# Weights in runs of four and a half rows: a decode kernel with attention and a small MLP, w3 loaded ahead of wq

## The chip, the core and the metric

The kernel runs on one core of a Trainium2 chip. Its engines are PE (TensorE: matrix products; PEld is its weight load), DVE (VectorE), ACT (ScalarE), POOL (GpSimd) and SP (SyncE, which here only issues DMA transfers); 16 DMA engines move the data. The metric is the device time of one execution in microseconds (us). It was measured three times for the kernel before, and one execution was profiled.

## The reference

Four sequences decode one token each. With D = 576, 32 query heads, 16 key/value heads of 128, F = 4608:

```python
x = A_x                                   # (4, 1, 576)
xn = _layernorm(x)
q = xn @ wq                               # (4, 4096): 32 heads of 128
k, v = last 2048 rows of the caches       # each (4, 16, 2048, 128), two query heads share one
A = softmax(q k^T * 128**-0.5) v @ wo     # (4, 576)
h = gelu(_layernorm(xn) @ w1)             # shifted by one or two tokens; with S = 1 that leaves zeros
x1 = xn + shifted(h) @ w2
B = x1 + gelu(_layernorm(x1) @ w3) @ w4   # w3: 576 x 4608, w4: 4608 x 576
out = x + A + B
```

All tensors are bfloat16. K and V are 33.6 MB each, the weights together 21.4 MB.

## The kernel before, in words

Each engine has its own program. The function add puts an operation into an engine's list with a key; each list is sorted by key, and semaphores carry the waits. So the order on an engine is set by the keys, and one late operation holds up all that are behind it. SP's list holds all transfers but x and the output, and a transfer that waits holds up those behind it too. Once issued, transfers run in the order of the queue, each split over the 16 DMA engines.

**SP's order.** wq in two transfers (keys -50, -49), w1, w2 and w3 in two each (-48 to -46), the first 24 of 36 rows of w4 (-45), then 16 K chunks of 2 MB (0 to 15), 8 V chunks of 4 MB, the rest of w4, and wo in five parts. K chunks go through a ring of four slots: chunk c waits until chunk c - 4 has been transposed (L296). Chunks 2 and 3 wait for q instead, since wq lies in their slots. V chunks 0 and 1 overwrite w3 and w4 and wait for MO0, the first part of the last MLP product. Later V chunks and wo wait for the products of V chunks that lay in their place.

**The weights before the change.** 576 rows don't divide by 128 partitions. The first 512 rows of wq, w1, w2 and w3 come as four rows in one run per partition (a run of 32 KB for wq, 36 KB for w3). The last 64 rows (rag_src, L209) come as 128 half rows in a transfer of their own (4 KB, 576 B, 576 B and 4.6 KB a run). x is transposed to match: four transposes of every fourth element (L334), and two more from ragsrc (L337), which holds the last 64 elements with zeros between them, once for the even partitions (first half of the columns) and once for the odd (second half).

**PE's order** (keys): q_zero; the transposes of xn and of its second layer norm; q (L370, 40 matmuls of four stationary columns, four side by side in column groups of the array, over two banks); the transposes of q (L383); the hidden layer (L404, two column groups); the product with w2 (L412, L413, two halves, the second waiting for DVE's sum of the first); the transposes of the third layer norm (L334); t1 (L431); a zero fill of banks (L358); h2 = x1n @ w3 (L444 and L450, three groups of 24 matmuls, waiting for w3); its transposes (L459); MO0 (L397, waiting for w4's first part); a zero fill of the score banks (L344). Then the loop over K: 64 transposes (L506) a chunk and 16 score matmuls (L513), with DVE (L490) and ACT (L489) copying the transposed blocks out. After it come the softmax, the loop over V (L574), and the products with w4's rest and wo (L397).

**DVE and ACT** in the prologue: the layer norms (ln_ops, L313; statistics, ACT's square root at L319, the scaling at L323, the two copies into ragsrc at L325 and L327), the copies of transposed x (L351, L426), of q (L376 on DVE, L377 on ACT) and into Qpad (L391), the sums x1 (L418), the gelus (L422, L423, L465), the copies of the transposed h2 (L468, L469) and of MO0 (L482, L483).

Of the kernel before, what the change touches and what calls it, by code (L numbers as in the profile page):

```python
# [37 lines left out]
def bass_parallel_sum__sliding_block_cached__mixer_s_mlp__decode_kernel(  # L38
# [32 lines left out]
    with ExitStack() as ctx:  # L71
# [6 lines left out]
        kring = sb("kring", [128, 4 * UE], BF16)  # L78
        vring = sb("vring", [128, 5 * UE], BF16)
        ktb = sb("ktb", [128, NKT * 1024], BF16)  # L80
        PT_t = sb("PT", [128, NT * 32], BF16)
# [6 lines left out]
        wqmain = kring[:, 2 * UE:4 * UE].rearrange("p (r n) -> p r n", r=4)  # L88
        wqrag = PT_t[:, 0:Hq * Dh // 2]
        w3main = vring[:, 0:4 * F].rearrange("p (r n) -> p r n", r=4)  # L90
        w4t = [vring[:, a:a + n * D].rearrange("p (r n) -> p r n", r=n) for a, n in ((4 * F, W4P[1]), (4 * UE, W4R - W4P[1]))]
        assert 4 * F + W4P[1] * D <= 4 * UE and (W4R - W4P[1]) * D + 1024 <= UE
# [9 lines left out]
        w1main = cut(4 * D).rearrange("p (r n) -> p r n", r=4)  # L102
        w1rag = cut(HALF)
        w2main = cut(4 * D).rearrange("p (r n) -> p r n", r=4)
        w2rag = cut(HALF)
        w3rag = cut(FH)
# [5 lines left out]
        PTv = PT_t[:].rearrange("p (q t b e) -> p q t b e", q=NVS, t=NTV, b=NPAIR)  # L112
# [9 lines left out]
        xn2_bf = sb("xn2_bf", [B, D], BF16)  # L122
        x1_bf = sb("x1_bf", [B, D], BF16)
        x1n_bf = sb("x1n_bf", [B, D], BF16)
        ragsrc = sb("ragsrc", [B, 3, 2, 128], BF16)
        xnT = sb("xnT", [128, 6, B], BF16)
        xn2T = sb("xn2T", [128, 6, B], BF16)
        x1nT = sb("x1nT", [128, 6, B], BF16)
        hs_inT = sb("hs_inT", [128, 6, B], BF16)
        hh_sb = sb("hh_sb", [32 + B, HALF], BF16)  # L130
        h2_sb = sb("h2_sb", [128, 3, 384], BF16)
        q_sb = vring[:, 5 * UE - 1024:5 * UE].rearrange("p (k x) -> p k x", k=2)
# [36 lines left out]
        Qps = [ps[:, 4, :], ps[:, 6, :]]  # L169
        QTps = ps[:, 0, :].bitcast(BF16).rearrange("p (k n j x) -> p k n j x", k=2, n=4, j=4)  # L170
        HSps = ps[0:B, 5, 0:HALF]
        HHps = [ps[32 * k:32 * k + B, 3, 0:HALF] for k in range(2)]
        H2ps = [ps[:, 4 + k, 0:384] for k in range(3)]
        H2Tps = [ps[:, k, :].bitcast(BF16).rearrange("p (n j x) -> p n j x", n=8, j=4) for k in range(2)]
        XTps = [ps[:, k, 0:12].bitcast(BF16).rearrange("p (c b) -> p c b", b=B) for k in range(3)]
# [33 lines left out]
        def rag_src(w_ap):  # L209
            return w_ap[512:576, :].rearrange("r (h n) -> (r h) n", h=2)  # L210
# [29 lines left out]
        P(lambda e: e.memset(ragsrc[:], 0.0), sig="rag_zero", key=-97)  # L240
# [24 lines left out]
        def mask_of(t, tag, view):  # L265
            add("dve", lambda e: e.tensor_reduce(out=t[:], in_=view, axis=AX.X, op=ALU.add), waits=["ident_f"], sig=tag, key=-8)
        mask_of(maskd, "maskd", ident_f[:].rearrange("p (t y) -> p t y", t=2))
# [45 lines left out]
        def ln_ops(idx, src, dst, first_waits, tag, k0):  # L313
# [9 lines left out]
            add("dve", lambda e: e.tensor_scalar(out=dst[:], in0=src[:], scalar1=mv[:, idx, 0:1], scalar2=rstd[:, idx:idx + 1],  # L323
                                                 op0=ALU.subtract, op1=ALU.mult), waits=[f"{tag}_rstd"], sig=f"{tag}_n", key=k0 + 0.04)
            add("dve", lambda e: e.tensor_copy(out=ragsrc[:, idx, 0, 0:128:2], in_=dst[:, 512:D]),  # L325
                waits=[f"{tag}_n"] + (["rag_zero"] if idx == 0 else []), key=k0 + 0.05)
            add("dve", lambda e: e.tensor_copy(out=ragsrc[:, idx, 1, 1:128:2], in_=dst[:, 512:D]),  # L327
                waits=["qpad_zero"] if idx == 1 else [], sig=tag, key=k0 + 0.05)

        def pe_xT(src, idx):  # L330
            def f(e):
                v = src[:, 0:512].rearrange("b (p r) -> b r p", r=4)
                for r in range(4):
                    e.transpose(XTps[idx][:, r, :], v[:, r, :], ident_bf[0:B, 0:B])  # L334
                ins = None
                for h in range(2):
                    ins = e.transpose(XTps[idx][:, 4 + h, :], ragsrc[:, idx, h, :], ident_bf[0:B, 0:B])  # L337
                return ins
            return f

# [7 lines left out]
        ln_ops(1, xn_bf, xn2_bf, ["ln1"], "ln2", -30)  # L348
        for idx, (src, tag, dst) in enumerate(((xn_bf, "ln1", xnT), (xn2_bf, "ln2", xn2T))):
            add("pe", pe_xT(src, idx), waits=["ident_bf", tag], sig=f"xT{idx}", key=-50 + idx)  # L350
            add("dve", lambda e, dst=dst, idx=idx: e.tensor_copy(out=dst[:], in_=XTps[idx]), waits=[f"xT{idx}"], sig=f"xnT{idx}",  # L351
                key=-29 + idx * 0.1)
# [8 lines left out]
        add("pe", pe_bank0(Qps), waits=["zeros_bf"], sig="q_zero", key=-51)  # L361

        def pe_q(r):
            def f(e):
                ins = None
                for k in range(8):
                    w, x_ = (wqmain[:, r, 512 * k:512 * (k + 1)], xnT[:, r, :]) if r < 4 else \
                        (wqrag[:, 512 * (k % 4):512 * (k % 4 + 1)], xnT[:, 4 + k // 4, :])
                    j = k % 4
                    ins = e.matmul(Qps[k // 4][32 * j:32 * j + B], lhsT=x_, rhs=w, start=False, stop=(r == 4),  # L370
                                   tile_position=(0, 32 * j), skip_group_check=True)
                return ins
            return f
        for r in range(5):
            add("pe", pe_q(r), waits=[ev_wq[r // 4], "xnT0"], sig="q" if r == 4 else f"q_{r}", key=-30 + r)
        add("dve", lambda e: e.tensor_copy(out=q_sb[:, 0], in_=Qps[0]), waits=["q"], sig="q_sb0", key=-11)  # L376
        add("act", lambda e: e.activation(out=q_sb[:, 1], in_=Qps[1], func=ACTF.Copy), waits=["q"], sig="q_sb1", key=-20)  # L377

        def pe_qT(k):
            def f(e):  # L380
                ins = None
                for n in range(4):
                    ins = e.transpose(QTps[:, k, n].rearrange("p j x -> p (j x)"), q_sb[:, k, 128 * n:128 * (n + 1)], ident_bf[:])  # L383
# [358 lines left out]
```

## Time and profile before

| | us |
|---|---|
| median of 3 runs | 214.5 (214.28 to 214.53) |
| the profiled execution | 214.28 |
| its span | 213.0 |
| PE busy | 170.8 (80%) |
| DVE busy | 118.6 (56%) |
| ACT busy | 61.3 (29%) |
| SP queue's packets, share of 16 DMA engines | 97.7% |
| bytes read | 88.49 MB |

The span runs from the first instruction of the program to the last; the time is 1.3 us longer. All positions are us from the span's start. A row of the timeline has the start, the duration, the engine, the line, the operation with out<-in and its count, and in brackets the idle time before it and what ended that. The chain of waits has start, duration and what it was. In a windows row stand the stretch, its length, then the busy time of PE, PEld, DVE, ACT and POOL with instruction counts, the clock granted to PE, the DMA engines' share and GB/s. A queue row has packets, MB, and the share of 16 engines' time.

### The profile page before, as it was taken

The numbers are of one execution on the slowest core, as the hardware profiler recorded it, in microseconds if no ns is written. First come the engines' busy times: TensorE is split into PE (matmuls) and PEld (weight loads), VectorE is DVE, ScalarE is ACT, GpSimd is POOL, SyncE is SP. The second block draws the span as 40 slices with busy tenths as digits, with TensorE's granted clock in tenths as the row PEclk, the third lists the DMA queues.
The fourth block names the chain that finished last, engine by engine and source line by source line (L and its number), as shares of the span: only waits on it lengthen the run. The fifth ranks groups of instructions, "written<-read, shape, count | busy, mean of one in ns | idle before, by whom it ended". The sixth has DMA issues, their size and how long they took to land.

```text
span 213.0 us, 4861 instructions
## 1 busy us (share of the span) xinstructions
PE 170.8 (80%) x2207; PEld 131.5 (62%) x2211; DVE 118.6 (56%) x172; ACT 61.3 (29%) x72; POOL 16.6 (8%) x39
## 2 busy tenths in 40 slices
PE   2037438679999999999999923899999869899965
PEld 0013106458877887778788802598888656788732
DVE  4964500047777776766676756999674570610110
ACT  2001402026666666655566645100000000000000
POOL 8993000000000000000000000000000000000000
PEclk9999757999999999999999985999999996999999
DMA  7999999999999999999999999999999999999993
GB/s 278 412 379 511 422 379 425 430 428 420 418 440 421 428 431 428 421 431 434 426 428 468 418 425 455 397 455 421 412 455 415 437 443 406 418 431 420 431 416 134
DMA packets 5786, 88.65 MB, mean 416 GB/s; under 512 B 648, under 2 KB 1040, under 8 KB 1808
## 3 DMA queue, kind: packets, MB, share of 16 engines
q1 hardware_dynamic: 5760, 88.49, 97.7%
q8 instruction: 8, 0.13, 0.3%
q14 instruction: 2, 0.02, 0.0%
q10 hardware_dynamic: 16, 0.01, 0.0%
HBM read 88.49 MB, written 0.00 MB: 415 GB/s over the span
## 4 chain that ended last, share of the span: by engine, by line
DMA 64%; PE 24%; DVE 9%; ACT 1%; issue 1%; SPq 0%
DMA kring<-in_A_k_cache_dram 40%; DMA vring<-in_A_wo_dram 12%; DMA vring<-in_A_v_cache_dram 12%; PE ps L574 11%; PE ps L506 7%; DVE xn_bf L323 4%; PE ps L513 2%; PE ps L370 2%; DVE vring L541 1%; DVE rmax L519 1%; DVE ktb L566 1%; PE ps L535 1%; DMA x_sb<-in_A_x_dram 1%; ACT ktb L489 0%; DVE stats L314 0%
## 5 line engine op out<-in xcount | busy, mean ns | idle before, releaser
L490 DVE COPY ktb<-ps 128x1024 bf16<-128x1024 bf16 x80 | 53.8, 690 | 24.5 <-PE ps L506 24.1
L506 PEld LDWEIGHTS ps<-perm_bf,kring 128*128 128x128 bf16 x1024 | 57.2, 98 | 11.6 <-issue 9.1
L506 PE MATMUL ps<-perm_bf,kring 128*128 128x128 bf16 x1024 | 62.6, 219 | 1.8 <-DMA kring<-in_A_k_cache_dram 1.1
L489 ACT ACTIVATE ktb<-ps 128x1024 bf16<-128x1024 bf16 x48 | 49.2, 1024 | 31.5 <-PE ps L506 30.5
L566 DVE TENSOR_TENSOR ktb<-PT,mH_bf 128x4096 bf16<-128x4096 bf16 x16 | 36.2, 2288 | 14.5 <-PE ps L574 14.5
L574 PE MATMUL ps<-vring,ktb 128*128 128x256 bf16 x256 | 30.3, 282 | 4.2 <-DMA vring<-in_A_v_cache_dram 3.3
L574 PEld LDWEIGHTS ps<-vring,ktb 128*128 128x128 bf16 x256 | 25.7, 101 | 8.3 <-issue 3.4
L574 PE MATMUL ps<-kring,ktb 128*128 128x256 bf16 x256 | 28.6, 273 | 0.9 <-DMA kring<-in_A_v_cache_dram 0.9
L574 PEld LDWEIGHTS ps<-kring,ktb 128*128 128x128 bf16 x256 | 25.0, 98 | 4.5 <-issue 1.2
L632 ACT ACTIVATE out_sb<-ps 4x288 bf16<-4x288 f32 x1 | 0.4, 400 | 76.3 <-PE ps L397 76.3
L513 PE MATMUL ps<-ktb,Qs 128*32 128x512 bf16 x272 | 17.8, 382 | 1.2 <-ACT ktb L489 1.2
L513 PEld LDWEIGHTS ps<-ktb,Qs 128*32 128x32 bf16 x272 | 5.8, 95 | 6.7 <-DVE ktb L490 1.3
L334 PE MATMUL ps<-ident_bf,xn_bf 4*128 4x4 bf16 x8 | 0.5, 169 | 11.2 <-DVE ragsrc L327 11.2
L535 PE MATMUL ps<-vring,pick_bf 128*32 128x256 bf16 x64 | 3.9, 411 | 6.4 <-DVE rinv L553 6.4
L592 DVE TENSOR_SCALAR tmp<-ps,maskd 128x128 f32<-128x128 f32 x2 | 0.7, 350 | 14.8 <-PE ps L574 14.8
L334 PEld LDWEIGHTS ps<-ident_bf,xn_bf 4*128 4x128 bf16 x8 | 0.4, 111 | 12.1 <-DVE ragsrc L327 8.7
L444 PE MATMUL ps<-vring,x1nT 128*4 128x384 bf16 x48 | 4.8, 486 | 3.7 <-DMA ktb<-in_B_w_dram 3.7
L323 DVE TENSOR_SCALAR xn_bf<-xn_bf,mv,rstd 4x576 bf16<-4x576 bf16 x1 | 7.1, 7102 | 0.0
L535 PEld LDWEIGHTS ps<-vring,pick_bf 128*32 128x32 bf16 x64 | 2.1, 118 | 8.2 <-DVE rinv L553 6.9
L468 DVE COPY h2T_sb<-ps 128x128 bf16<-128x128 bf16 x1 | 0.2, 226 | 12.4 <-PE ps L459 12.4
L246 POOL MEMSET ktb<- 128x8192 bf16 x1 | 6.9, 6925 | 0.0
L397 PE MATMUL ps<-vring,ORT 128*4 128x288 bf16 x64 | 4.6, 286 | 2.4 <-DMA vring<-in_A_wo_dram 2.2
(115 smaller groups left out, 87.1 us busy)
## 6 DMA issues: line engine op xcount, KB each, us to landing
kring<-in_A_k_cache_dram SPq DMA_DIRECT2D x16, 2048.0 KB, 14.7
vring<-in_A_v_cache_dram SPq DMA_DIRECT2D x4, 4096.0 KB, 24.6
kring<-in_A_v_cache_dram SPq DMA_DIRECT2D x3, 4096.0 KB, 34.0
vring<-in_B_w_dram SPq DMA_DIRECT2D x1, 4608.0 KB, 24.7
kring<-in_A_wq_dram SPq DMA_DIRECT2D x1, 4096.0 KB, 12.2
kring<-in_A_v_cache_dram SPq DMA_DIRECT2D x2, 2048.0 KB, 27.3
vring<-in_B_w_dram SPq DMA_DIRECT2D x1, 3456.0 KB, 34.7
vring<-in_A_wo_dram SPq DMA_DIRECT2D x1, 1872.0 KB, 30.4
```

What stands on the lines that cost most here:

```text
L246: P(lambda e: e.memset(ktb[:, NKT // 2 * 1024:NKT * 1024], 0.0), key=-92, inc=(("E", LB - 2), 1))
L323: add("dve", lambda e: e.tensor_scalar(out=dst[:], in0=src[:], scalar1=mv[:, idx, 0:1], scalar2=rstd[:, idx:idx + 1], op0=ALU.subtract, op ...
L370: ins = e.matmul(Qps[k // 4][32 * j:32 * j + B], lhsT=x_, rhs=w, start=False, stop=(r == 4), tile_position=(0, 32 * j), skip_group_check=True)
L397: return e.matmul(ACC[h], lhsT=lhsT, rhs=rhs, start=start, stop=stop, tile_position=(0, 32 * h), skip_group_check=True)
L444: ins = e.matmul(H2ps[k][32 * j:32 * j + B].rearrange("b (p t) -> b p t", t=3), lhsT=x1nT[:, r, :], rhs=w3main[:, r, :].rearrange("x (p t) ...
L489: return "act", lambda e: e.activation(out=ktbuf[:, n % NKT], in_=tb[n % 4], func=ACTF.Copy)
L490: return "dve", lambda e: e.tensor_copy(out=ktbuf[:, n % NKT], in_=tb[n % 4])
L506: ins = e.transpose(tb[j % 4][:, t, :], kslot_t(k)[:, 8 * kb + t, :], perm_bf[:])
L513: ins = e.matmul(Sps[32 * u:32 * u + 32, q, :].rearrange("p (t i) -> p t i", t=16), lhsT=Qs[:, k, 32 * u:32 * u + 32], rhs=ktgrp[:, (4 * k ...
L535: ins = e.matmul(ps[32 * j:32 * j + 32, 4 + qt, 256 * ih:256 * (ih + 1)].rearrange("p (t a e) -> p t a e", a=NPAIR, e=2), lhsT=pick_bf[:, ...
L566: return lambda e: e.tensor_tensor(out=PTpad[:, n % 4], in0=PTv[:, qt, NH * h:NH * (h + 1), bp, :].unsqueeze(2).to_broadcast([128, NH, NX, ...
L574: ins = e.matmul(ps[:, 0, 0:256], lhsT=PTpad[:, 2 * (k % 2) + h, 2 * g:2 * g + 2].rearrange("p t h e -> p (t h e)"), rhs=vslot(k)[:, Dh * ...
```

## The change

wq, w1, w2 and w3 come in one transfer each. 576 rows are 64 groups of nine, so a partition takes half a group: four and a half rows in one run (36 KB of wq, 5.2 KB of w1 and of w2, 41.5 KB of w3). In such a run the halves of a row lie in turn on even and odd places, the other way round on even and odd partitions. So each matmul runs over a half row (nine of them), with eight stationary columns of x: four with x on the even partitions and zeros on the odd, four the other way. The one set of four outputs is the first half of the columns, the other the second. xs holds these columns; two DVE operations write them from the transposed x with the mask par. x is first laid out in pairs (xp).

With that, q has 36 matmuls of eight columns into one bank instead of 40 of four into two, one copy (on ACT) and four transposes; the hidden layer 9 in one column group instead of 10 in two; the product with w2 9 + 9 instead of 5 + 5; h2 two groups of 36 (320 and 256 columns) instead of three of 24; and the transposition of h2 is 18 products with a slice of the identity instead of 9 transposes. ragsrc, its copies and its memset on POOL are gone.

On SP w3 goes first (key -50), then wq (-49), w1, w2 and w4. q's last part no longer has a transfer of its own to wait for. w4's first part starts a little later in its buffer, since w3 takes more of it. The buffer PT moves to the end of kring, and wq's runs reach into it.

```diff
-        def rag_src(w_ap):
-            return w_ap[512:576, :].rearrange("r (h n) -> (r h) n", h=2)
+        def runs(w_ap):
+            return w_ap.rearrange("(m e) n -> m (e n)", e=9).rearrange("m (a x) -> (m a) x", a=2)
...
-        ev_wq = [add_dma([(kring[:, 2 * UE:4 * UE], A_wq[0:512, :].rearrange("(p r) n -> p (r n)", r=4))], "wq", (), -50),
-                 add_dma([(wqrag, rag_src(A_wq))], "wqr", (), -49)]
-        ev_w1 = add_dma([(w1main, B_w1[0:512, :].rearrange("(p r) n -> p r n", r=4)), (w1rag, rag_src(B_w1))], "w1", (), -48)
-        ev_w2 = add_dma([(w2main, B_w2[0:512, :].rearrange("(p r) n -> p r n", r=4)), (w2rag, rag_src(B_w2))], "w2", (), -47)
-        ev_w3 = add_dma([(vring[:, 0:4 * F], B_w3[0:512, :].rearrange("(p r) n -> p (r n)", r=4)), (w3rag, rag_src(B_w3))],
-                        "w3", (), -46)
+        ev_wq = add_dma([(wq_t, runs(A_wq))], "wq", (), -49)
+        ev_w1 = add_dma([(w1_t, runs(B_w1))], "w1", (), -48)
+        ev_w2 = add_dma([(w2_t, runs(B_w2))], "w2", (), -47)
+        ev_w3 = add_dma([(w3_t, runs(B_w3))], "w3", (), -50)
...
+        def xs_ops(idx, k0):
+            for a in range(2):
+                add("dve", lambda e, a=a: e.tensor_scalar(
+                        out=xs_t[:, idx, 2 * B * (1 - a):2 * B * (11 - a)].rearrange("p (r v b) -> p r v b", v=4, b=B)[:, :, 0:4:3, :],
+                        in0=XTps[idx].unsqueeze(2).to_broadcast([128, 5, 2, B]), scalar1=par[:, a:a + 1], scalar2=None, op0=ALU.mult),
+                    waits=([f"xT{idx}"] + ([] if idx else ["par"])) if a == 0 else [], sig=f"xs{idx}{a}", key=k0 + 0.01 * a)
...
+        def pe_q(s_):
             def f(e):
                 ins = None
+                for j in range(4):
+                    ins = e.matmul(Qps[32 * j:32 * j + 2 * B], lhsT=x_at(0, s_), rhs=wq_t[:, NQ // 2 * s_ + 512 * j:NQ // 2 * s_ + 512 * (j + 1)],
+                                   start=False, stop=(s_ == 8), tile_position=(0, 32 * j), skip_group_check=True)
                 return ins
...
         def pe_hh(e):
             ins = None
+            for s_ in range(9):
+                ins = e.matmul(HHps, lhsT=x_at(1, s_), rhs=w1_t[:, HALF * s_:HALF * (s_ + 1)], start=(s_ == 0), stop=(s_ == 8))
             return ins
...
+                for s_ in range(9):
+                    w = w3_t[:, FH * s_:FH * (s_ + 1)].rearrange("x (p t) -> x p t", t=W4R)
+                    for j in range(4):
+                        ins = e.matmul(H2ps[k][32 * j:32 * j + 2 * B].rearrange("b (p t) -> b p t", t=n), lhsT=x_at(2, s_),
+                                       rhs=w[:, :, 9 * j + t0:9 * j + t0 + n], start=False, stop=(s_ == 8),
+                                       tile_position=(0, 32 * j), skip_group_check=True)
...
+            for k, (t0, n) in enumerate(TS):
+                for t in range(n):
+                    for g in range(2):
+                        ins = e.matmul(H2Tps[64 * g:64 * (g + 1), t0 + t], lhsT=h2_v[k].rearrange("q (p t) -> q p t", t=n)[:, :, t],
+                                       rhs=sel[:, :, B * g:B * (g + 1)], start=True, stop=True, tile_position=(0, 64 * g),
+                                       skip_group_check=True)
```

More of the change, by code (lines that the diff above doesn't have):

```diff
@@ L121, in bass_parallel_sum__sliding_block_cached__mixer_s_mlp__decode_kernel @@
         xn_bf = sb("xn_bf", [B, D], BF16)
-        xn2_bf = sb("xn2_bf", [B, D], BF16)
+        xp_bf = sb("xp_bf", [B, 3, 5 * 128], BF16)
         x1_bf = sb("x1_bf", [B, D], BF16)
[L124 to L132, printed above, removed]
+        xs_t = sb("xs", [128, 3, 22 * B], BF16)
+        par = sb("par", [128, 2], FP32)
+        hs_inT = sb("hs_inT", [128, 9, 2, B], BF16)
+        hh_sb = sb("hh_sb", [2 * B, HALF], BF16)
+        h2_sb = sb("h2_sb", [128, 64 * 9], BF16)
+        q_sb = vring[:, 5 * UE - 512:5 * UE]
         h2T_sb = sb("h2T_sb", [128, W4R, B], BF16)
@@ L347, in bass_parallel_sum__sliding_block_cached__mixer_s_mlp__decode_kernel @@
         ln_ops(0, x_sb, xn_bf, [ev_x], "ln1", -40)
[L348 to L352, printed above, removed]
+        ln_ops(1, xn_bf, None, ["ln1_n"], "ln2", -30)
+        for idx, tag in enumerate(("ln1", "ln2")):
+            add("pe", pe_xT(idx), waits=["ident_bf", tag], sig=f"xT{idx}", key=-50 + idx)
+            xs_ops(idx, -29 + idx * 0.1)
         def pe_bank0(banks):
@@ L360, in pe_bank0 @@
             return f
-        add("pe", pe_bank0(Qps), waits=["zeros_bf"], sig="q_zero", key=-51)
-        def pe_q(r):
+        add("pe", pe_bank0([Qps]), waits=["zeros_bf"], sig="q_zero", key=-51)
+        def pe_q(s_):
             def f(e):
                 ins = None
[L366 to L371, printed above, removed]
-                return ins
-            return f
@@ L374, in bass_parallel_sum__sliding_block_cached__mixer_s_mlp__decode_kernel @@
[L374 to L383, printed above, removed]
-                return ins
-            return f
```

138 lines of the change are left out of this document (64 added, 74 removed).

## Prediction

> **What bounds the kernel now.** I read the page first: the busy share of the DMA engines in 40 slices, then the queues.
>
> ```profile
> span 213.0 us, 4861 instructions
> ...
> DMA  7999999999999999999999999999999999999993
> ...
> q1 hardware_dynamic: 5760, 88.49, 97.7%
> q8 instruction: 8, 0.13, 0.3%
> ```
>
> From the second slice to the one before last the DMA engines are full. SyncE's queue (q1) moves 88.49 MB in 5760 packets, and their time is 97.7% of all that 16 engines have. PE comes second with 80%, so I ask next which of the two is waited for, in the chain of waits:
>
> ```profile
> 18.53 40.55 DMA kring<-in_A_k_cache_dram
> ...
> 59.12 1.51 PE ps L506 x24
> 60.63 0.98 PE ps L513 x16
> 61.61 2.35 PE ps L506 x40
> 63.96 0.02 issue
> 63.98 14.67 DMA kring<-in_A_k_cache_dram
> ...
> 185.11 25.35 DMA vring<-in_A_wo_dram
> ```
>
> The chain names long transfers, but in each of them the transfer spends most of its time queued behind others. A K chunk is issued at 63.98 and lands 14.67 us later, which is three chunks of 4.89 us: it stood behind two. PE needs 63.96 - 59.12 = 4.84 us for one. DMA is the bound, PE is 0.05 us a chunk faster, and no queue runs empty. The last piece of wo lands at 185.11 + 25.35 = 210.46, and the rest of the 213.0 is the end of the output.
>
> So two things can move the end: the time that the DMA engines need for their bytes and packets, and a hole in their work. One more view, the windows at the end, shows that the engines don't finish together:
>
> ```profile
> 209.00:210.00 1.00, 0.65 (x12) 0.35 (x10) 0.00 (x0) 0.00 (x0) 0.00 (x0) 1.00 0.51 203
> 210.00:211.00 1.00, 0.71 (x12) 0.26 (x8) 0.00 (x0) 0.00 (x0) 0.00 (x0) 1.00 0.12 40
> ```
>
> The last two columns are the DMA share and the GB/s: with shares of 0.51 and 0.12, half of the engines' work is over by about 209.5, the last of it at 210.5. The slowest engine sets the time, and the fastest are up to some 2 us ahead of it.
>
> **Part 1, the transfers.** The bytes stay. Four small transfers go (the last 64 rows of wq, w1, w2 and w3), each of 128 runs and 16 closing packets: 576 packets, 36 on each engine. What a packet costs beside its bytes I take from the queue rows of two stretches, 12 to 17.5 us (weights, small runs among them) and 60 to 80 us (K, 16 KB runs), and the rate from a window with 32 KB runs:
>
> ```profile
> q1 hardware_dynamic: 752, 2.44, 109.2%
> ```
> ```profile
> q1 hardware_dynamic: 583, 8.50, 100.0%
> ```
> ```profile
> 140.00:160.00 20.00, 19.95 (x181) 17.58 (x181) 17.11 (x8) 0.00 (x0) 0.00 (x0) 1.00 1.01 435
> ```
>
> At 435 / 16 = 27.2 bytes per ns, the first stretch has 1.092 x 16 x 5.5 = 96.1 us of engine time, of which the bytes need 89.7: 6.4 us over 752 packets, 8.5 ns each. The second has 320 us, the bytes 312.5: 13 ns each. 36 packets are then 0.31 to 0.46 us per engine. From below it may be nothing, since packets overlap (a share of 109.2%). From above: wq's large part lands at 13.0 (rows below) and w3's small one at 31.3 (L444 waits for it until 31.34). The 7.16 MB between take 16.5 us at 435 GB/s, so 1.85 us are lost there to everything: packets, seams, and an instruction fetch of 16 KB that falls into them. I take **0.35 us**, near the lower packet price, because the stretch with small runs is the nearest row.
>
> The Trainium skill (DMA: Bandwidth & Descriptors, Anatomy of one DMA) gives a fixed cost of about 2 us per DMA beside the bytes, and says that most of it is waiting for the completion. If it added up in a full queue, four fewer would be worth 8 us; the first row above speaks against that (2.44 MB in 5.5 us is 444 GB/s, though several transfers end there).
>
> **Part 2, w3 ahead of wq: when PE can start.** Everything that PE does before the K chunks now waits for wq behind w3. How late is that?
>
> ```profile
> 0.80 0.37 SPq L205 DMA_DIRECT2D kring<-in_A_wq_dram  x1
> ```
> ```profile
> kring<-in_A_wq_dram SPq DMA_DIRECT2D x1, 4096.0 KB, 12.2
> ```
>
> 4.19 MB landed at 0.80 + 12.2 = 13.0, as if full rate began at 3.4. w3 and wq are 10.03 MB: 23.0 us, so wq lands at about **26.4**. w1 and w2 follow by 29.5, w4's first part by 37.7, K chunk 0 before 44.5. The work of PE until the first K transposition, which was spread over two waits for DMA, now runs in one piece after 26.4. Its steps, from PE's timeline:
>
> ```profile
> 14.20 3.27 PE L370 MATMUL ps<-kring,xnT 128*4 128x512 bf16 x32
> 17.30 0.60 PE L370 MATMUL ps<-PT,xnT 128*4 128x512 bf16 x8
> 18.70 0.62 PE L383 MATMUL ps<-ident_bf,vring 128*128 128x128 bf16 x8 [0.81 <-DVE vring L376]
> 19.26 0.78 PE L404 MATMUL ps<-ktb,xn2T 128*4 128x288 bf16 x10
> 19.87 0.65 PE L412 MATMUL ps<-ktb,hs_inT 128*4 128x288 bf16 x4
> ...
> 26.48 1.14 PE L358 MATMUL ps<-zeros_bf 128*128 128x384 bf16 x3
> 31.34 1.12 PE L444 MATMUL ps<-vring,x1nT 128*4 128x384 bf16 x10 [3.73 <-DMA ktb<-in_B_w_dram]
> ...
> 37.09 0.68 PE L459 MATMUL ps<-ident_bf,h_sb 128*128 128x128 bf16 x9 [0.61 <-ACT h_sb L465]
> 39.55 3.10 PE L397 MATMUL ps<-vring,h2T_sb 128*4 128x288 bf16 x48 [1.78 <-DMA vring<-in_B_w_dram]
> 42.82 0.81 PE L344 MATMUL ps<-zeros_bf 128*128 128x512 bf16 x3 [0.16 <-issue]
> 44.54 1.51 PE L506 MATMUL ps<-perm_bf,kring 128*128 128x128 bf16 x24 [0.92 <-DMA kring<-in_A_k_cache_dram]
> ```
> ```profile
> 37.95 0.16 DVE L469 COPY h2T_sb<-ps 128x16 bf16<-128x16 bf16 x1
> ```
>
> Without the waits: q to hidden layer 14.20 to 19.26, 5.06; on to the end of the zero fill, 27.62, 8.36; h2 31.34 to 37.09, 5.75; its transposition until the copy's end at 38.11, 1.02; MO0 and zero fill 39.55 to 43.63, 4.08. Sum 24.3.
>
> The new matmuls change this. q has 36 for 40 and four transposes for eight: 4 x 0.05 and 4 x 0.06 less, and one copy on ACT, 0.5 less with the shorter wait. The hidden layer loses its two column groups: 9 in a row at 0.121 (L412: (0.65 - 0.286) / 3) for 10 at 0.061 (L404 takes 0.61 until L412), +0.5; w2's product takes 9 + 9 for 5 + 5, 8 x 0.121 = +1.0. Two small copies per layer norm go, -0.2; the zero fill has 576 columns for 1152, -0.5; h2 streams 72 matmuls of 20736 columns for 23040, -0.5. Its transposition takes 18 small matmuls for 9, +0.5. Together +0.3: 24.6 us, so the K transpositions start at 26.4 + 24.6 = **51.0**, 6.5 us later than the 44.54 of before.
>
> What do 6.5 us cost? Chunk 4 is issued when chunk 0 is transposed, and an issue needs time until its data flow:
>
> ```profile
> 49.40 20.08 SPq L205 DMA_DIRECT2D kring<-in_A_k_cache_dram  x5
> ```
> ```profile
> 0.81 1.73 DMA x_sb<-in_A_x_dram
> ```
>
> The issue comes 49.40 - 44.54 = 4.86 after PE's start, so now at 55.9. The small load of x was issued and landed within 1.73 us, so data flow at most 1.7 us after an issue, and I estimate not before 1.1: at 57.0 to 57.6. The slowest engine is busy with chunk 3 until 59.07 - 0.35 = 58.7; chunk 3's landing is 18.53 + 40.55 = 59.08 in the chain. So the engine that sets the time has 1.1 to 1.7 us to spare, while the fastest may idle for under 1 us. That costs nothing, but the reserve is thin. Later the lag does no harm: PE regains 0.05 us a chunk, and the V stage, where wo is issued 25.35 us ahead of its landing, has far more in its queue. K chunks 2 and 3 wait for q, now at about 30, with w4 and chunks 0 and 1 queued until 47. DVE, ACT and POOL do their added or saved work (xp, xs, par, the dropped memset) while wq is still on its way, between 5 and 26 us; without that cover it would add about 1 us to PE's start, still inside the reserve.
>
> **Sum.** -0.35 + 0 on the profiled execution's own 214.28, which is the fastest of three; on the median of 214.5 it gives 214.15, so I forecast **214.2**. About 0.2% (0.43 us) is what a measurement here can tell from no change; the forecast lies just inside.
>
> **Rivals.**
>
> *PE comes too late (slower).* One place: the issue of K chunk 4. From a PE start of about 52.3 on, each us of delay is a us of hole in all engines. PE idles for 20 us now and may run q and what follows at half speed; the row
>
> ```profile
> L370 PE MATMUL ps<-kring,xnT x32: 380/631/634, 14.2 to 17.1; 128*4 128x512 bf16 x32
> ```
>
> shows q beginning at 631 ns a matmul and ending at 380. If the clock stays low through w1 and w2, 27 matmuls x 0.12 = +3.2 us, start 54.2, hole 1.9 us: 214.2 + 1.9 = 216.1. If only q is slow to its end, +0.5, nothing is lost. For it: each of my steps can be off by 0.3. Against: q warmed the clock within its own 3.3 us before. The Trainium skill (TensorE: Matmul & The Clock Gate, Part 1: The HAM clock gate) has the clock halved after an idle window of about 3.4 us and restored after a busy one, with a window that runs freely; by that, q alone would be slow, at most. Chance 0.28, times 214.3 to 216.2.
>
> *The seams cost more than packets.* If most of the 1.85 us between 13.0 and 31.3 belonged to small runs and to the fetch among them, the time would be 212.7; with half of it 213.6. Against: the fetch still has to come, on some engine. Chance 0.15.
>
> *Small packets are free.* They overlap, and nothing that sets the end has changed: 214.5. Chance 0.08.
>
> *Two instruction fetches meet on one engine.* The 8 fetches shift in time with PE. The 1.85 us less packets leave some 1.5 for one of them on the engine that it hits, so two on one engine give 215.7. Chance 0.05.
>
> **How the numbers follow.** The forecast has 0.44; of it 0.20 lies beyond 0.2% (the packets at 13 ns or more), 0.24 within. Faster: 0.20 + 0.15 = 0.35. Same: 0.24 + 0.08 + 0.05 of a small hole = 0.37. Slower: 0.23 + 0.05 = 0.28. The range, 213.2 to 215.8, takes in half of the seams and a hole of 1.6 us; the likeliest case alone is 213.9 to 214.5.
>
> **What would show it.** The first K transposition at about 51.0, wq's landing at 26.4, K chunk 3 landing some 0.35 us earlier than 59.08, and the DMA row without a digit below 9 near slices 11 and 12. A gap there, with chunk 4's landing later than before, is the first rival; wo landing over 1 us earlier is the second. The sum is wrong if wq lands much after 26.4 or if a run of 41 KB moves at less than 27 bytes per ns.

## The result, and the profile after

The changed kernel takes a median of 217.34 us (217.13 to 217.89, 5 runs), the kernel before 214.5 us (214.28 to 214.56, 5 runs): a ratio of 1.0144, interval 1.0133 to 1.0154. It is slower by 3 us; the forecast was 214.2 us, and 215.8 the top of its range. The profiled execution took 217.13 us, with a span of 215.9. All ratios leave out slow runs, over 1.5% above the fastest of the same kernel; there are two of them, of the ten runs of the kernel called e5 below (217.91 and 218.0).

The page of the changed kernel, in the parts that the prediction showed of before:

```profile
span 215.9 us, 4862 instructions
...
DMA  7989999999999999999999999999999999999991
GB/s 247 476 384 437 407 470 414 422 422 425 378 361 386 413 431 437 431 434 428 425 424 461 419 449 425 434 419 440 425 425 440 419 437 431 407 428 429 422 404 57
...
q1 hardware_dynamic: 5184, 88.49, 97.0%
```

The packets are fewer by 576 and the bytes the same, as expected. The DMA row says almost nothing: near the K chunks in question every digit is 9. The row below it does: slices 11 to 13 (54 to 70 us) moved 378, 361 and 386 GB/s, and from slice 14 to 39 it is 404 to 461 again. So a busy DMA engine need not be a fast one, and the bytes have to be read beside the share. Windows of the changed kernel (last two columns: DMA share, GB/s):

```profile
56.00:58.00 2.00, 2.00 (x36) 1.25 (x34) 1.44 (x3) 1.53 (x2) 0.00 (x0) 1.00 0.91 320
...
62.00:64.00 2.00, 2.00 (x39) 1.58 (x32) 1.02 (x2) 0.60 (x2) 0.00 (x0) 1.00 1.01 320
68.00:70.00 2.00, 2.00 (x40) 2.00 (x38) 1.80 (x4) 1.39 (x2) 0.00 (x0) 1.00 0.79 311
56.00:74.00 18.00, 18.00 (x312) 15.00 (x310) 13.03 (x23) 11.45 (x12) 0.00 (x0) 1.00 0.98 377
74.00:180.00 106.00, 94.38 (x1303) 78.75 (x1301) 77.84 (x97) 38.92 (x45) 0.00 (x0) 0.97 1.01 431
```

The last two windows of the kernel before:

```profile
56.00:74.00 18.00, 17.74 (x300) 14.30 (x292) 12.69 (x22) 10.83 (x12) 0.00 (x0) 1.00 1.00 424
74.00:180.00 106.00, 93.58 (x1232) 76.62 (x1231) 74.17 (x90) 36.78 (x42) 0.00 (x0) 0.96 1.01 431
```

From 74 us on both kernels move 431 GB/s. All that is lost is lost in 18 us: (424 - 377) x 18 / 431 = 2.0 us on the mean of the 16 engines. The last of them loses more: by the landings in the trace chunk 6 comes 1.6 us later than before on its first engine (73.50 for 71.94) and 3.0 us later on its last (76.71 for 73.75). The slow places are three: where the engines come to chunk 4 (56.5), to chunk 5 (62.3) and to chunk 6 (67.8). By the landings on the first engine these chunks take 5.66, 5.49 and 5.49 us, and 4.89 before the change. In the trace's packet records a 16 KB packet takes 0.61 us as a rule, and many take 0.9 to 2.0 us there. The same records split the loss between 55 and 76 us: per engine 0.4 us passed without any packet, nearly all of it at the start of chunk 4, where 7 of the 16 engines had one around 56.9 us, and 1.8 us were lost to packets that took longer than 0.61; in the kernel before it is 0.0 and 0.1.

PE's timeline of the changed kernel, up to its first K transposition:

```profile
26.91 3.80 PE L373 MATMUL ps<-kring,xs 128*8 128x512 bf16 x36 [19.19 <-DMA kring<-in_A_wq_dram]
...
31.74 1.27 PE L401 MATMUL ps<-ktb,xs 128*8 128x288 bf16 x9
32.85 1.27 PE L409 MATMUL ps<-ktb,hs_inT 128*4 128x288 bf16 x9
34.65 1.26 PE L409 MATMUL ps<-ktb,hs_inT 128*4 128x288 bf16 x9 [0.54 <-DVE x_bf L415]
38.91 0.27 PE L334 MATMUL ps<-ident_bf,xp_bf 4*128 4x4 bf16 x5 [2.99 <-DVE xp_bf L318]
...
40.72 4.27 PE L442 MATMUL ps<-vring,xs 128*8 128x320 bf16 x72
45.49 0.79 PE L455 MATMUL ps<-ident_bf,h_sb 128*64 128x16 bf16 x18 [0.50 <-ACT h_sb L461]
46.78 3.10 PE L396 MATMUL ps<-vring,h2T_sb 128*4 128x288 bf16 x48 [0.49 <-DVE h2T_sb L464]
49.81 1.04 PE L351 MATMUL ps<-zeros_bf 128*128 128x512 bf16 x4
50.72 1.46 PE L500 MATMUL ps<-perm_bf,kring 128*128 128x128 bf16 x23
```

The issues of SyncE (a row joins four of them), and the chain of waits:

```profile
55.58 14.58 SPq L201 DMA_DIRECT2D kring<-in_A_k_cache_dram  x4
```
```profile
1.24 25.63 DMA kring<-in_A_wq_dram
26.91 3.83 PE ps L373 x36
...
53.21 3.71 PE ps L500 x64
56.91 0.98 PE ps L507 x16
57.89 3.71 PE ps L500 x64
...
186.33 26.98 DMA vring<-in_A_wo_dram
```

In the chain of before a K chunk waited for its bytes; now PE's own work stands there without a gap, 3.71 + 0.98 = 4.69 us a chunk, behind wq's landing at 26.87. The end is still wo's landing: 186.33 + 26.98 = 213.31, and before 210.46.

### The profile page after: what moved, and what is told of

It reads as the page before. It is cut to its first block, busy times and chain, and to the rows that moved or that the text cites. A ratio compares the mean times of both kernels' runs of the same rounds, so it can differ in the third digit from the quotient of the medians.

```text
span 215.9 us, 4862 instructions
## 1 busy us (share of the span) xinstructions
PE 166.0 (77%) x2214; PEld 130.2 (60%) x2214; DVE 112.3 (52%) x169; ACT 58.6 (27%) x70; POOL 15.7 (7%) x38
## 4 chain that ended last, share of the span: by engine, by line
PE 55%; DMA 36%; DVE 6%; ACT 1%; issue 1%; SPq 0%
PE ps L500 27%; DMA vring<-in_A_wo_dram 12%; DMA kring<-in_A_wq_dram 12%; DMA vring<-in_A_v_cache_dram 12%; PE ps L568 10%; PE ps L507 8%; PE ps L442 2%; PE ps L373 2%; PE ps L396 2%; DVE vring L535 1%; PE ps L409 1%; DVE rmax L513 1%; DVE ktb L560 1%; PE ps L529 1%; PE ps L401 1%
## 5 line engine op out<-in xcount | busy, mean ns | idle before, releaser
L500 PE MATMUL ps<-perm_bf,kring 128*128 128x128 bf16 x1024 | 60.4, 219 | 0.0
L483 ACT ACTIVATE ktb<-ps 128x1024 bf16<-128x1024 bf16 x48 | 47.6, 1023 | 28.9 <-PE ps L500 28.9
L560 DVE TENSOR_TENSOR ktb<-kring,mH_bf 128x4096 bf16<-128x4096 bf16 x16 | 36.2, 2288 | 12.7 <-PE ps L568 12.7
L568 PE MATMUL ps<-vring,ktb 128*128 128x256 bf16 x256 | 28.6, 273 | 4.0 <-DMA vring<-in_A_v_cache_dram 2.2
L568 PEld LDWEIGHTS ps<-vring,ktb 128*128 128x128 bf16 x256 | 24.9, 98 | 7.4 <-issue 3.3
L373 PE MATMUL ps<-kring,xs 128*8 128x512 bf16 x36 | 3.8, 604 | 19.2 <-DMA kring<-in_A_wq_dram 19.2
L373 PEld LDWEIGHTS ps<-kring,xs 128*8 128x8 bf16 x36 | 1.1, 119 | 21.3 <-DMA kring<-in_A_wq_dram 19.3
L390 DVE COPY Qpad<-ps 128x32 bf16<-128x32 bf16 x4 | 0.5, 184 | 23.5 <-PE ps L384 23.5
L379 ACT ACTIVATE vring<-ps 128x512 bf16<-128x512 f32 x1 | 0.6, 597 | 24.5 <-PE ps L373 24.5
L334 PE MATMUL ps<-ident_bf,xp_bf 4*128 4x4 bf16 x15 | 0.8, 163 | 8.2 <-DVE xp_bf L318 5.0
```

The costliest lines, as they stand in the source:

```text
L373: ins = e.matmul(Qps[32 * j:32 * j + 2 * B], lhsT=x_at(0, s_), rhs=wq_t[:, NQ // 2 * s_ + 512 * j:NQ // 2 * s_ + 512 * (j + 1)], start=Fal ...
L483: return "act", lambda e: e.activation(out=ktbuf[:, n % NKT], in_=tb[n % 4], func=ACTF.Copy)
L500: ins = e.transpose(tb[j % 4][:, t, :], kslot_t(k)[:, 8 * kb + t, :], perm_bf[:])
L560: return lambda e: e.tensor_tensor(out=PTpad[:, n % 4], in0=PTv[:, qt, NH * h:NH * (h + 1), bp, :].unsqueeze(2).to_broadcast([128, NH, NX, ...
L568: ins = e.matmul(ps[:, 0, 0:256], lhsT=PTpad[:, 2 * (k % 2) + h, 2 * g:2 * g + 2].rearrange("p t h e -> p (t h e)"), rhs=vslot(k)[:, Dh * ...
```

## The experiments

Two theories at first. **Lateness** (L in the expectations): w3 ahead of wq starts PE's K loop 6.2 us later (50.72 for 44.54), so chunk 4 is issued at 55.58 for 49.40, and that is the whole loss. **Layout or order** (R, the rival): the 41 KB runs of w3, or w3's place in the queue, leave the DMA engines slower or uneven. Later a finer question: does chunk 4 cost only once an engine has run dry (**dry**), or already when it is issued a short time ahead of that (**short lead**)? In the later expectations S is the short lead, D the dry engine, and O the order itself.

All kernels, by the moment at which chunk 4 was issued in the profiled execution. The first engine lands its part of chunk 3 at 56.8 to 57.3 in all of them; the lead is 57.0 less the issue. GB/s is that of 56 to 74 us in the same execution, the time the median of all runs.

| kernel | w3 first | chunk 4 issued | lead | GB/s | us (lowest to highest, runs) |
|---|---|---|---|---|---|
| before | no | 49.40 | 7.6 | 424 | 214.5 (214.28 to 214.56, 5) |
| e1: wq first | no | 49.73 | 7.3 | 428 | 214.22 (214.07 to 214.29, 10) |
| e11: e1, 9 idle matmuls | no | 51.32 | 5.7 | 427 | 214.15 (214.10 to 214.37, 10) |
| e14: w3 first, PE work cut | yes | 52.73 | 4.3 | 422 | 214.50 (214.31 to 214.65, 10) |
| e13: w3 first, h2 cut | yes | 53.72 | 3.3 | 426 | 216.90 (214.46 to 217.49, 6) |
| e12: e1, chunk 4 alone waits | no | 54.19 | 2.8 | 407 | 215.26 (214.26 to 216.41, 10) |
| e8: e1, all chunks wait | no | 54.33 | 2.7 | 385 | 217.08 (217.04 to 217.11, 2) |
| e6: e1, 18 idle matmuls | no | 54.43 | 2.6 | 391 | 215.75 (214.38 to 216.22, 5) |
| e10: w3 first, w2 cut, idles | yes | 54.77 | 2.2 | 390 | 216.05 (215.77 to 216.81, 4) |
| e2: before, with w3 first | yes | 54.98 | 2.0 | 401 | 216.03 (215.74 to 216.91, 4) |
| e9: w3 first, idles | yes | 55.23 | 1.8 | 389 | 216.47 (214.98 to 217.87, 10) |
| e5: e1, 27 idle matmuls | no | 55.36 | 1.6 | 385 | 216.83 (214.21 to 218.00, 10) |
| after | yes | 55.58 | 1.4 | 377 | 217.34 (217.13 to 217.89, 5) |
| e4: w3 first, w2 cut | yes | 56.26 | 0.7 | 365 | 218.01 (1) |
| e7: e1, chunk 4 alone waits longer | no | 57.26 | -0.3 | 382 | 216.58 (216.18 to 216.99, 2) |
| e3: e1, 39 idle matmuls | no | 58.25 | -1.3 | 339 | 219.37 (1) |

**The order alone, both ways (e1, e2).** e1 puts wq first and w3 behind w2 in the changed kernel; e2 puts both transfers of w3 ahead in the kernel before.

```diff
-        ev_wq = add_dma([(wq_t, runs(A_wq))], "wq", (), -49)
+        ev_wq = add_dma([(wq_t, runs(A_wq))], "wq", (), -51)
...
-        ev_w3 = add_dma([(w3_t, runs(B_w3))], "w3", (), -50)
+        ev_w3 = add_dma([(w3_t, runs(B_w3))], "w3", (), -46)
```
```diff
-                        "w3", (), -46)
+                        "w3", (), -51)
```

> The changed kernel with only SP's order put back: wq first, then w1, w2, w3, w4. Theory L (PE starts the K loop so late that chunk 4 is issued when most DMA engines have run dry; the restart and what follows cost about 3 us): PE starts the K loop when chunk 0 lands, at about 43, chunk 4 is issued by 49, no dip in the DMA row, and what is left is the gain of 0.35 us of fewer packets: 214.1. Rival R (the long runs themselves, 41 KB and 36 KB, or the eight-column matmuls are what costs): stays at 217 or more.

> The kernel before with only w3's two transfers put ahead of wq, its runs and matmuls unchanged. Theory L: wq lands near 27 and the K loop starts at about 51, so 217 (216.5 to 218). Rival R: order alone costs nothing, 214.5.

e1 took 214.22 us, a ratio to the kernel before of 0.9988 (0.9979 to 0.9998); e2 216.03, a ratio of 1.0087 (1.0063 to 1.0111). So the new runs and the new matmuls are not to blame: with wq first they gain a little, and the old runs lose with w3 first as well. The windows of e1 show no loss, those of e2 a loss at chunks 5 and 6 only:

```profile
56.00:74.00 18.00, 17.76 (x303) 14.46 (x296) 12.81 (x23) 10.88 (x12) 0.00 (x0) 1.00 1.01 428
74.00:180.00 106.00, 93.81 (x1227) 76.71 (x1226) 73.99 (x90) 36.63 (x42) 0.00 (x0) 0.95 1.01 430
```
```profile
56.00:60.00 4.00, 4.00 (x72) 3.24 (x70) 2.76 (x6) 2.28 (x4) 0.00 (x0) 1.00 1.03 432
61.50:63.00 1.50, 1.50 (x32) 1.10 (x21) 0.66 (x2) 0.11 (x1) 0.00 (x0) 1.00 1.04 339
67.00:68.50 1.50, 1.50 (x31) 1.50 (x29) 1.05 (x2) 0.81 (x1) 0.00 (x0) 1.00 0.91 262
```

**PE late without any change of order (e3, e5, e6, e11).** Idle matmuls on zeros stand ahead of the K loop of e1; 39, 27, 18 and 9 of them.

```diff
+        add("pe", lambda e: pe_idle(39)(e), key=-0.5)
```

> wq first with the new runs, and 39 matmuls of 512 columns on zeros (8.4 us) put on PE right ahead of the K loop, so that the loop starts at about 50.7 as in the changed kernel. Theory L: the start alone decides, so 217 again, with the dip in DMA throughput from 57 us on. If the order of the weights in the queue did it in another way (uneven DMA engines, a different place in the queue): 214 to 215.

> wq first, new runs, and 27 idle matmuls on PE ahead of the K loop (39 had brought it to 53.4), so that the loop starts at about 50.7, as in the changed kernel. If the start of the K loop is the whole cause, 217.3 as there (216.8 to 217.9). If w3 ahead of wq costs anything by itself, less.

> The same with 18 idle matmuls, start at about 48.8: chunk 4 is issued at 53.5 and its data can flow at 54.9, 2 us before the first engine is dry. Theory D (what costs is the restart of dry engines): 214.2. Theory S (a K chunk whose transfer starts within about 3 us of its issue is slow at its beginning, dry or not): two or three slow beginnings of 0.4 us, about 215.2.

> The changed kernel with wq first and 9 idle matmuls ahead of the K loop: start at about 47.0, chunk 4 issued at 51.9, 5 us ahead of need. Theory S: 214.1 to 214.4, as without idles (214.22), since the lead is over 3.6 us. If every us of PE's start costs from the beginning (a straight line from 44.87 and 214.22 to 49.58 and 215.75): 214.9.

The 39 idles put the start at 53.40 where 50.7 was aimed at, so e3 answers the question of a late start, and e5 that of the start of the changed kernel: started at 50.51 with wq first, it takes 216.83 us, a ratio of 1.008 (1.0044 to 1.0116). That is 1.9 us more than e1 by the ratio and 2.6 by the medians, of the 3.1 us that the changed kernel is behind e1. So lateness alone is enough for most of the loss, whatever the order. e6 had been expected to cost nothing by the prediction's account, since its chunk 4 is issued 2.5 us ahead of the first dry engine; it costs about 1 us, 215.75 and a ratio of 1.0042 (1.0014 to 1.0069). e11 costs nothing, 0.9992 (0.9982 to 1.0002): a straight price per us of PE's start is out, and there is an edge.

**Less PE work with w3 first (e4).**

```diff
-                for s_ in range(9):
-                    ins = e.matmul(HSps, lhsT=hs_inT[:, s_, h, :], rhs=w2_t[:, HALF * s_:HALF * (s_ + 1)], start=(s_ == 0), stop=(s_ == 8))
+                for s_ in range(1):
+                    ins = e.matmul(HSps, lhsT=hs_inT[:, s_, h, :], rhs=w2_t[:, HALF * s_:HALF * (s_ + 1)], start=True, stop=True)
```

> The changed kernel with w3 first, leaving out 16 of the 18 matmuls of w2's product, all of which multiply zeros. PE's prologue is 1.9 us shorter, the K loop starts at about 48.8, chunk 4 is issued at 53.7 and its data can flow at 55.0, before any engine is dry (56.9). Theory L: no dip, 214.1 to 214.4. Rival R: 217.

A miss: the K loop started later, at 51.40, not earlier. PE's timeline of e4 shows where the saved time went:

```profile
32.16 2.32 PE L401 MATMUL ps<-ktb,xs 128*8 128x288 bf16 x9
...
38.66 0.29 PE L334 MATMUL ps<-ident_bf,xp_bf 4*128 4x4 bf16 x5 [3.00 <-DVE xp_bf L318]
```

The nine matmuls of the hidden layer take 2.32 us for the 1.27 of the changed kernel, about half the pace. They stand ahead of the product that was cut, so the cut is not the reason; e14 below, which leaves w2's product whole, has them at the same pace:

```profile
32.02 2.32 PE L401 MATMUL ps<-ktb,xs 128*8 128x288 bf16 x9
```

Then PE waits 3.00 us for the layer norm as before, and from there to the end of h2 it takes 7.0 us for 6.1. The time, 218.01, is one more point on the same line.

**Chunk 4 alone, and all chunks (e7, e8, e12).** In e1 one chunk, or each, waits for more transpositions than it must (8 belong to a chunk: T7 is the last of chunk 0), while PE starts as early as in e1. The three lines are those of e7, e8 and e12.

```diff
-            w = [t_done(c - N_CB)] if c >= N_CB else (["q"] if c >= 2 else [])
+            w = ["T19"] if c == N_CB else [t_done(c - N_CB)] if c >= N_CB else (["q"] if c >= 2 else [])
...
+            w = [t_done(c - N_CB + 1)] if c >= N_CB else (["q"] if c >= 2 else [])
...
+            w = ["T15"] if c == N_CB else [t_done(c - N_CB)] if c >= N_CB else (["q"] if c >= 2 else [])
```

> wq first, PE in time, and K chunk 4 alone waits for three blocks of chunk 2, so that it is issued at about 56.6 and its data flow at 58.0, about 1 us after most engines are dry; chunks 5 and 6 are issued right behind it and long ahead of their start. Theory D: the restart itself makes what follows slow, 216.5 or more, with slow beginnings at chunks 5 and 6. Theory S: only chunk 4 suffers, by the hole on the slowest engine or little more, 214.3 to 215.2, and chunks 5 and 6 run at full rate.

> wq first, PE in time, and every K chunk from 4 on waits for the transposition of one chunk later, so that each starts some 2.7 to 3.4 us after its issue; no engine is dry. Theory D: 214.2. Theory S: several chunks with a slow beginning, 216 to 219.

> The changed kernel with wq first, in which chunk 4 alone waits for one more chunk of transpositions: issued at about 54.3, 2.6 us ahead of the first dry engine (56.9), every later chunk as early as before. Theory S: one slow beginning at 56.5 to 60, and 214.8 to 215.6, between the 214.22 of no wait and the 216.58 of the kernel in which chunk 4 is issued at 57.26. Rival (only an engine that has in fact run dry costs something): 214.2, since 54.3 is ahead of 56.9.

e7 is the plain hole (216.58, ratio 1.0098, 1.0074 to 1.0122). It met neither expectation in full: the time is that of D, but no chunk behind the hole begins slowly, as in S. Its windows:

```profile
57.50:58.00 0.50, 0.50 (x13) 0.50 (x10) 0.45 (x1) 0.29 (x1) 0.00 (x0) 1.00 0.23 98
58.00:58.50 0.50, 0.50 (x13) 0.50 (x10) 0.34 (x1) 0.50 (x1) 0.00 (x0) 1.00 0.00 0
58.50:59.00 0.50, 0.50 (x11) 0.39 (x8) 0.50 (x2) 0.23 (x1) 0.00 (x0) 1.00 1.60 524
60.00:74.00 14.00, 11.76 (x177) 9.31 (x178) 7.35 (x14) 6.69 (x8) 0.00 (x0) 0.88 1.01 426
```

Issued at 57.26, chunk 4 flows from 58.6 to 58.9 on, 1.3 to 1.7 us later by its packets, and nearly at full rate (first packets of 0.64 to 1.09 us, the next of 0.61 to 0.74); the next chunks, issued at 57.83 and 59.04 and so far ahead, lose nothing. The end still moves by all of the hole: wo lands 2.1 us later than in e1. The engine that was last with chunk 3 (58.9, 2.0 us behind the first) had no hole to speak of, and yet it did not keep the end where it was. The landings in the trace suggest why: after the hole 15 of the 16 engines land chunk 4 within 0.44 us of each other, and the sixteenth 1.83 us after the first. A fetch of 16 KB of instructions started at 62.83. The records don't name the engine that it fell on, but in the kernel before, too, one more engine lands 1.0 to 1.4 us late after each of the first fetches. So these fetches (8 in the run, about 1.0 us each) seem to come to ever other engines, and the late engine of one moment isn't the one of the end.

e12 was meant to separate dry from short lead. Its chunk 4 was issued at 54.19, 2.8 us ahead, and the chunks after it as early as ever:

```profile
56.00:58.00 2.00, 2.00 (x40) 1.57 (x32) 0.99 (x2) 0.60 (x2) 0.00 (x0) 1.00 0.85 303
58.00:60.00 2.00, 1.96 (x36) 1.79 (x33) 1.80 (x4) 1.63 (x2) 0.00 (x0) 1.00 1.02 377
62.00:64.00 2.00, 1.76 (x32) 1.58 (x29) 1.79 (x3) 1.23 (x2) 0.00 (x0) 1.00 1.00 418
56.00:74.00 18.00, 16.15 (x274) 12.99 (x267) 11.23 (x20) 9.49 (x11) 0.00 (x0) 1.00 0.99 407
```

One slow beginning and none after it, with a part of the engines empty at first (share 0.85) and long packets on others (1.2 to 1.6 us in the trace): 215.26 us, a ratio of 1.0036 (1.0017 to 1.0055), where dry was expected to give 214.2. The packets say that it doesn't quite separate the two: three engines had none from 56.75 to 58.25, up to 4 us after the issue, so some ran dry in spite of the lead. e2 does separate them. Counted as above between 55 and 76 us, an engine of e2 is never without a packet, and it loses 1.2 us to long packets alone; in e12 the two parts are 0.3 and 0.7 us, in e5 0.2 and 1.6, in e8 0.8 and 1.5, in e7 1.6 and 0.4. In e8 the leads came out at 2.7, 3.4, 3.4 and 1.9 us for chunks 4 to 7 (from chunk 5 on to the first landing of the chunk before): slow beginnings stand at 56.5 and at 72.3, none at the two chunks with 3.4, and the time is 217.08. So a chunk that is issued under about 3 us before its turn often begins slowly, and each such chunk adds to the loss.

**w3 first, but early (e9, e10, e13, e14).** These ask whether the order costs anything by itself. Twelve idle matmuls keep PE busy while it waits for the third layer norm; e10 cuts w2's product besides (as e4), e13 the h2 product, e14 also the product with w4's first part.

```diff
+        add("pe", lambda e: pe_idle(12)(e), key=-21)
...
-                for s_ in range(9):
+                for s_ in range(1):
                     w = w3_t[:, FH * s_:FH * (s_ + 1)].rearrange("x (p t) -> x p t", t=W4R)
...
-        add("pe", pe_MO(0, 0, W4P[1]), waits=[ev_w4[0], "h2T", "t1acc"], sig="MO0", key=-10)
+        add("pe", pe_MO(0, W4P[1] - 3, W4P[1]), waits=[ev_w4[0], "h2T", "t1acc"], sig="MO0", key=-10)
```

> The changed kernel with w3 still first, and 12 idle matmuls on PE in the stretch in which it waits for the third layer norm, to keep the granted clock up for the h2 product (which took 4.27 us for 72 matmuls there). If the h2 product then takes about 2.8 us, the K loop starts at 49.2 to 49.7 instead of 50.72 and chunk 4 is issued at 54.1 to 54.6, 2.5 to 3 us ahead of the first dry engine. Theory S (a chunk issued less than about 3 us ahead of the moment at which an engine runs dry starts slowly, and the slow start is never made up): 215.4 to 216.3, by the row of the wq-first kernel that starts at 49.58 (215.75). Theory O (it is the order of the weights itself, whenever PE starts): unchanged, 217.3. If the idle matmuls run at half clock and delay PE, the start is later than 50.7 and this run says nothing on either.

> As the run before, and w2's product cut to one of its nine steps in both halves (this leaves out 16 of 18 matmuls of that product; the transfer of w2 stays). w3 is still first. The K loop should start at about 47.2 to 48.0 and chunk 4 be issued at 52.1 to 52.9, over 4 us ahead of the first dry engine. Theory S: no slow stretch at chunks 4, 5 and 6, and 214.0 to 214.6, the time of the kernel with wq first (214.22) with w3 first. Theory O: 216.5 or more.

> The kernel with w3 first and 12 idle matmuls, and the h2 product cut to one of its nine steps (this leaves out 64 of its 72 matmuls; the transfer of w3 stays, and still goes ahead of wq). The h2 product took 3.56 us in the run with the idles, so the K loop should start at about 47.2 instead of 50.37 and chunk 4 be issued at about 52.1, 4.8 us ahead of the first dry engine. Theory S (only a short lead of the issue costs; the order of the weights costs nothing by itself): no slow stretch at chunks 4, 5 and 6, and 214.0 to 214.5, the time of the kernels with wq first (214.15 and 214.22). Theory O (the order of the weights itself costs, by what it leaves behind in the DMA engines): 216 or more, with slow stretches whatever the lead.

> As the run before (w3 first, 12 idle matmuls, the h2 product cut to 8 of its 72 matmuls), and the product with the first part of w4 cut to 6 of its 48 matmuls (both are left out of the result; every transfer stays). That product took 4.78 us there, so the K loop should start at about 44.6 instead of 48.85, as early as with wq first (44.87), and chunk 4 be issued at about 49.5, 7 us ahead of the first dry engine. Theory S: no slow stretch in any run, all runs within 214.0 to 214.6, none of the scatter of the run before (214.46 to 217.49). Theory O (the order itself costs in some executions, whatever the lead): scatter to 216 or more stays.

e9 started at 50.37 and e10 at 49.91, far less early than aimed at: in e9 q began 0.2 us later and took 0.2 longer, and in e10 the hidden layer ran at half the pace again (2.32 us); they are two more points near the edge (ratios 1.0102, 1.007 to 1.0133, and 1.0076, 1.0059 to 1.0092). e13 (start 48.85) stands on the edge itself: its profiled execution took 214.46 us with 426 GB/s and no slow beginning, with w3 first, and four of its six runs 216.8 to 217.5. e14 got a start of 47.14, not 44.6, but chunk 4 out at 52.73:

```profile
56.00:58.00 2.00, 2.00 (x39) 1.99 (x37) 1.80 (x5) 1.60 (x2) 0.00 (x0) 1.00 0.97 397
56.00:74.00 18.00, 18.00 (x311) 14.98 (x309) 13.37 (x24) 11.86 (x12) 0.00 (x0) 1.00 1.00 422
74.00:180.00 106.00, 94.28 (x1281) 79.04 (x1279) 75.68 (x92) 36.97 (x43) 0.00 (x0) 0.97 1.01 432
```

All ten runs lie within 0.4 us, and the ratio is 1.0006 (0.9996 to 1.0016). The order by itself costs some 0.3 us at most by these medians (214.5 beside e1's 214.22), and theory O falls. What these 0.3 us are is not shown.

## Why the prediction was wrong

**Right: what PE does and when.** wq was forecast to land at 26.4 and landed at 26.87; the piece of PE's work behind it was put at 24.6 us and took 50.72 - 26.91 = 23.8; the first K transposition came at 50.72 for 51.0, the issue of chunk 4 at 55.58 for 55.9. The piece came out partly by luck: its listed changes add up to -0.1 us, not +0.3, q up to the hidden layer took 4.8 us where its terms give 4.1, and the rest took 19.0 for 20.0. Data flow 1.3 to 1.7 us after an issue (e7), inside the 1.1 to 1.7 that was estimated. K chunk 3, which was to land 0.35 us before 59.08, landed last at 59.20, though on its first engine at 56.86 for 57.27. No digit of the DMA row fell below 9 at slices 11 and 12; that this would clear the forecast was itself a mistake, since the digit counts busy engines and not bytes.

**Right in kind: the transfers.** Forecast -0.35 us, with bounds of 0 and -1.85. e1 holds the whole change but the order, and its ratio of 0.9988 (0.9979 to 0.9998) is -0.26 us of 214.44 (-0.45 to -0.04); e11 gives the same within its interval. So the rival with much dearer seams (212.7 or 213.6) is out. The Trainium skill (DMA: Bandwidth & Descriptors, Anatomy of one DMA) puts a fixed cost of about 2 us on a DMA issued from GpSimd, most of it the wait for its completion. Here SyncE issued, and four DMAs fewer in a full queue were worth 0.26 us, so in this queue no such cost added up.

**The step that failed** is the sentence on chunk 4: "So the engine that sets the time has 1.1 to 1.7 us to spare, while the fastest may idle for under 1 us. That costs nothing, but the reserve is thin." It put the edge at a PE start of 52.3, which is an issue at 57.2. The runs put it between an issue at 52.73 (e14, no loss) and 53.72 (e13, loss in four runs of six), some 4 us earlier. The idle time of the fastest engines was forecast rightly (0.4 us on the mean). Two things were wrong in the rest:

- A queue was taken to run at full rate as long as something is in it. But chunks that were issued 1.4 to 3.1 us ahead of their turn often began at 260 to 390 GB/s, with shares from 0.8 to 1.1 (e12, e8, e6, e2, and the windows of the changed kernel). This is the larger part: 1.8 of the 2.2 us per engine that the changed kernel lost there.
- The last engine was taken to be the one that sets the end. But a hole in the other 15 counts too: in e7 the last engine had nearly none, and the end moved by 2.1 us. That the next instruction fetch falls on another engine and makes it the last is the likely reason, by the landings of e7.

**Also wrong: "Later the lag does no harm: PE regains 0.05 us a chunk".** The lead of chunk 5 and 6 was short as well, since PE needs 4.69 us a chunk and a chunk 4.89 us of DMA: 0.2 us of lead come back per chunk, and each slow beginning adds its own delay. Chunk 5 was issued at 60.26 for a turn at 62.5, chunk 6 at 64.95 for one at 68.0, both began slowly, and at chunk 7 (69.63 for 73.5) the lead was long enough. Three slow beginnings make the 3 us; one alone (e12) makes 1.0 (215.26 - 214.22).

**The first rival** named the right place, the issue of chunk 4, and the right sign, with a price that begins only at a start of 52.3, 1.6 us after the start that cost 3 us. Its story of a clock that stays low was not needed: the forecast start came true. Its mild case did come: q ran slow nearly to its end, as the row shows (shortest, median and longest matmul in ns):

```profile
L373 PE MATMUL ps<-kring,xs x36: 421/631/634, 26.9 to 30.3; 128*8 128x512 bf16 x36
```

The clock fell again after the wait for the layer norm, as two windows of the changed kernel show (PEclk is the third number from the end of a row). The same two of e9, where idle matmuls fill the wait, stand below them:

```profile
36.00:41.00 5.00, 1.55 (x19) 0.56 (x23) 3.44 (x9) 1.89 (x3) 0.00 (x0) 0.96 1.02 435
41.00:46.00 5.00, 4.50 (x86) 2.56 (x80) 0.00 (x0) 0.82 (x2) 0.00 (x0) 0.70 0.99 419
```
```profile
36.00:41.00 5.00, 4.10 (x25) 1.49 (x23) 3.49 (x9) 1.89 (x3) 0.00 (x0) 1.00 0.98 419
41.00:46.00 5.00, 4.35 (x90) 3.12 (x90) 0.03 (x1) 0.82 (x2) 0.00 (x0) 1.00 1.01 426
```

The h2 product took 4.27 us in the one and 3.56 in the other. The Trainium skill (TensorE: Matmul & The Clock Gate, Part 1: The HAM clock gate) says that the clock is halved after an idle window of about 3.4 us. The halving agrees: the trace's clock records of the changed kernel have half speed from 40.60 to 44.01, which makes the 0.70. But the 3.4 us ahead of it were not all idle: the wait was 2.99 us, and 1.3 us of small matmuls followed. How much work a window may hold and still count as idle, the runs don't show.

**What stays open.** Why packets take 0.9 to 2.0 us for 0.61 at the start of a chunk with a short lead, while a chunk that finds most engines empty starts at nearly full rate (e7), the runs don't show. Nor do they show what decides in a single execution: near the edge the same kernel takes 214.2 in one run and 217.2 in another (e5), and only one execution of each was traced. Two chunks with leads of 2.0 to 2.2 us began at full rate (chunk 4 of e2, chunk 5 of e3), so the lead sets how likely a slow beginning is, not whether it comes.

**The best version** is e1, the new transfers with wq first: 214.22 us, 0.12% below the kernel before (interval 0.02% to 0.21%) and 3.1 us below the changed kernel.

## What to carry to other kernels

In a kernel whose DMA queue is full, the lead of each issue over the moment at which the engines reach it is a resource: work it out for every chunk of a ring, and before an edit delays the consumer that frees the buffers, see that more than 4 us of it stay (here 4.3 cost nothing, 3.3 and less mostly 1 to 3 us). Reserves of the slowest engine alone are none. When a full queue loses time, read GB/s by windows, not the busy share, and compare the same window of both kernels.

## What the runs showed of the hardware that was not expected

- A chunk of 2 MB that had been issued 1.4 to 3.1 us before its turn often began at 260 to 390 GB/s for 1 to 4 us, in e2 without any engine running empty; the engines counted as busy at the same time (share 1.01 at 320 GB/s in the changed kernel).
- A chunk issued after most engines had run dry started 1.3 to 1.7 us after its issue, at nearly full rate (e7). With the engines still busy, three of them were without a packet until 4 us after the issue (e12).
- A fetch of 16 KB of instructions takes about 1.0 us on a DMA engine. In the kernel before, one engine lands 1.4 us behind the others after the first fetch (at 31.30, the next at 29.91), and four of them when chunk 3 lands (58.6 to 59.1, the others 57.3 to 57.6); in the full queue none catches up.
- The nine matmuls of the hidden layer took 1.27 us in some executions and 2.32 in others of kernels with the same work ahead of them (the changed kernel, e9 and e13; e4, e10 and e14).
